# Layer 1's hidden-side products of chunks 0 to 2 as seven block products on quartered blocks

## The chip, the cores and the metric

The kernel runs on one core of a Trainium2 chip. The metric is the device time of one execution in microseconds (us), with all inputs in the chip's memory (HBM) at the start and the output there at the end. The kernel before has a median of 1414.64 us over 3 runs (1414.49 to 1414.83).

## The reference

Two layers are applied to x, 2048 rows by 512 columns. Each adds a Fourier mixing of the normalized rows, and then a small MLP with shifts along the sequence. Cut to what matters:

```python
def _A_ref(x, dft_seq_re, dft_seq_im, dft_hid_re, dft_hid_im):
    a = jnp.einsum("bsd,ed->bse", x, dft_hid_re)
    b = jnp.einsum("bsd,ed->bse", x, dft_hid_im)
    y = jnp.einsum("ts,bse->bte", dft_seq_re, a) - jnp.einsum("ts,bse->bte", dft_seq_im, b)
    return y

def _B_ref(x, w1, w2, w3, w4):
    h = _gelu(_layernorm(x, axis=-1) @ w1)
    hs = ...            # h with its four column groups shifted by +1, -1, +2, -2 rows, @ w2
    x1 = x + hs
    h2 = _gelu(_layernorm(x1, axis=-1) @ w3) @ w4
    return x1 + h2

x = A_x
for _ in range(2):
    x = x + _A_ref(_layernorm(x, axis=-1), ...)
    x = x + _B_ref(_layernorm(x, axis=-1), B_w1, B_w2, B_w3, B_w4)
```

The change concerns the product with the hidden-side matrices (`dft_hid_re`, `dft_hid_im`) in the second layer, which the kernel calls layer 1.

## The kernel before

**Numbers.** Every fp32 operand of a matmul is held as two numbers, a high part (a cast to fp32r by ScalarE, ACT) and a low part (the difference, by VectorE, DVE). A product is three matmuls on TensorE (PE), high by high, high by low and low by high; `mm3` issues them (lines 303 to 305). So each operand costs a cast on ACT and a subtraction on DVE ahead of its first use.

**Transform.** The rows are worked in four chunks c = 0 to 3 of 512. First come the products with the sequence-side matrices (`in_ws`), whose results are the real and imaginary blocks `re0, re1, im0, im1` in the tile `rr`, each 128 partitions by 2 by 512 columns, high and low part side by side. Then comes the product of these blocks with the hidden-side matrix `in_hs`. The sequence-side work of a chunk has two phases:

- The **x phase** (`x_phase`) has eight pairs k = 0 to 7, each with an even step 2k (12 matmuls of 512 columns, called the wide step in the prediction) and an odd step 2k + 1 (6 matmuls, the narrow step). Steps are numbered 0 to 15.
- The **y phase** (`y_phase`) has 16 steps of 12 matmuls.

The hidden-side products of chunk c - 1 stand in the x phase of chunk c, as eight pieces of 512 KB, in pairs given by the table `HAT`. `hid` does one piece: 2 x 2 products by `mm3`, 12 matmuls of 512 columns, into the banks `PD`. Four pieces make half of the chunk's rows, and `add_y` adds them to x and collects the row sums in the same DVE operation (line 607). Those of chunk 3 come after its y phase, by `hid` too.

**How operands come.** A list `items`, made before anything is issued, says in which order pieces of `in_ws` and `in_hs` are used. A piece is brought by a DMA that SyncE (SP) issues (line 223) into one of four raw buffers of 512 KB (two more, `wide`, toward the y phase). From there it goes to one of four ring slots of 1024 KB: `stage_one` casts the high part on ACT (line 247 for a whole piece, a "plain" item; for an odd step, a "one" item, a DVE difference comes first, line 249), and `stage_two` makes the low part on DVE (line 266). `stream` is called at each step and keeps the ring full, so DMAs, casts and low parts run up to four places ahead of PE. A raw buffer is free for the next DMA when its last reader is done, and a DMA that has to wait for that holds up all those behind it on SP.

**Other work in the x phase.** The table `late` maps a step number to pieces of work that `run_late` issues at that step: the sums and the high and low parts of the last chunk's `re` and `im` blocks, and the normalization sums of its rows. `hook(i)` loads x rows and stores results at fixed steps. Each engine works its own instructions in the order in which the program issues them.

**MLP.** `by_pairs` works two chunks at a time. `first_pair` does chunks 0 and 1. The second pair (chunks 2 and 3) in layer 0 is a loop over five rounds p, each with seven block products `prod` (banks b1, b6, b5, b2, b7, b4, b3 in turn out of four), whose sums `u, v, x, y` DVE adds. Between them `w4_part` does the product with w4, and the list `bg`, one entry at a time by `one()`, prepares the rows of layer 1. At a round's end `w3_load` brings the weight block (1792 KB) of the round after the next. In the next round, two sums read b4 and b3 of the round before it is over:

```python
            prod(b4, w, 6, "t4")
            add(v, b4, v, ALU.subtract)
            low2 = gelu_high(h4[2 * (p % 2) + 1], v)
            prod(b3, w, 2, "22")
            add(x, x, b3)
```

The banks are `bk[(2 + 7 * p + i) % 4]`, so b4 of a round is the bank that the third product of the next round writes.

## Time and profile before

| | before |
|---|---|
| median of 3 runs | 1414.64 us |
| the profiled execution | 1414.44 us |
| its span, first to last instruction | 1412.5 us |
| PE busy | 1407.2 us |
| DVE busy | 1190.1 us |
| ACT busy | 765.3 us |
| GpSimd (POOL) busy | 96.5 us |
| traffic with HBM | 260.70 MB read, 54.26 MB written, 223 GB/s |
| layer 1, x phase of chunk 1 | 792.77 to 847.17, 54.40 us |
| layer 1, y phase of chunk 1 | 847.17 to 890.70, 43.53 us |
| layer 0, MLP of chunks 2 and 3 (second pair) | 603.22 to 716.27, 113.05 us |

The profile is of one execution. A row of a group gives line, engine, operation, what is written and read, the shape, how many, the busy time and the mean ns of one, and the idle time ahead of them with what ended it. A row of a stretch of time gives the stretch, its length, and the busy time and number of instructions of PE, its weight loads (PEld), DVE, ACT and POOL, the clock that PE was granted (1.00 is full), the DMA share and GB/s. A row of the order of time gives the start, the duration and, in brackets, the idle time ahead with what ended it. Matmuls overlap: one shows 0.39 us at 512 columns, and the distance between starts is what it costs PE.

### The profile page before, as it was taken

What the parts mean: (1) busy time and instruction counts of PE and PEld (TensorE: products, weight loads), DVE (VectorE), ACT (ScalarE), POOL (GpSimd) and SP (SyncE); (2) the same over time, 40 slices, a digit from 0 to 9 for tenths busy, and PEclk for the clock granted to TensorE, in tenths of its full rate; (3) what the DMA queues carried; (4) which work ended last, traced back from release to release, by engine and by line L of the source; (5) the groups of instructions that cost most, each with busy time, mean ns of one, the idle gap of its engine ahead of it and who ended that gap; (6) DMA issues with size and microseconds to landing.
All of it is one profiled execution on the core that took longest, in us unless ns stands there. A gap on an engine that the chain in (4) does not pass through costs nothing.

```text
span 1412.5 us, 18484 instructions
## 1 busy us (share of the span) xinstructions
PE 1407.2 (100%) x6669; PEld 1181.7 (84%) x6669; DVE 1190.1 (84%) x1684; ACT 765.3 (54%) x1072; POOL 96.5 (7%) x105
## 2 busy tenths in 40 slices
PE   9999999999999999999999999999999999999998
PEld 8888888888888888988888888888888888899887
DVE  7988998999988789856789979879889788897776
ACT  6765565556566645434555544555555666454351
POOL 2100220400001100000000000000000020000000
PEclk9999999999999999999999999999999999999999
DMA  8878868778874848864656476565577457677864
GB/s 295 307 235 300 262 206 274 241 239 293 284 229 131 281 148 262 269 235 168 216 164 216 146 224 211 160 214 178 188 248 248 136 143 244 193 247 257 295 208 158
DMA packets 158907, 316.18 MB, mean 224 GB/s; under 512 B 10848, under 2 KB 78816, under 8 KB 156896
## 3 DMA queue, kind: packets, MB, share of 16 engines
q1 hardware_dynamic: 158816, 315.01, 67.8%
q8 instruction: 52, 0.85, 0.2%
q14 instruction: 39, 0.32, 0.1%
HBM read 260.70 MB, written 54.26 MB: 223 GB/s over the span
## 4 chain that ended last, share of the span: by engine, by line
PE 95%; DVE 3%; ACT 1%; issue 1%; DMA 0%; SPq 0%; POOL 0%; DVEq 0%; ACTq 0%; POOLq 0%
PE psd L303 10%; PE psd L304 10%; PE psd L305 10%; PE psa L303 8%; PE psa L305 8%; PE psa L304 8%; PE psb L303 7%; PE psb L304 7%; PE psb L305 7%; PE psc L304 7%; PE psc L303 7%; PE psc L305 7%; DVE rest L500 1%; DVE z3turned L643 1%; DVE uv L500 0%
## 5 line engine op out<-in xcount | busy, mean ns | idle before, releaser
L247 ACT CAST ring<-raw 128x1024 fp32r<-128x1024 f32 x127 | 132.6, 1051 | 70.4 <-PE psd L305 33.7
L266 DVE TENSOR_TENSOR ring<-raw,ring 128x1024 fp32r<-128x1024 f32 x126 | 153.3, 1219 | 14.3 <-ACT ring L247 14.3
L354 POOL TENSOR_TENSOR rows<-ve,mhalf 128x4 f32<-128x4 f32 x16 | 47.2, 2952 | 702.9 <-DVE ve L353 702.9
L303 PE MATMUL psd<-ring,rr 128*128 128x512 f32 x208 | 80.9, 389 | 0.0
L304 PE MATMUL psd<-ring,rr 128*128 128x512 f32 x208 | 80.9, 389 | 0.0
L305 PE MATMUL psd<-ring,rr 128*128 128x512 f32 x208 | 80.9, 389 | 0.0
L322 POOL TENSOR_TENSOR rs<-ve,mhalf 128x2 f32<-128x2 f32 (+2 forms) x33 | 28.4, 862 | 411.8 <-DVE nb L321 392.9
L266 DVE TENSOR_TENSOR ring<-ring1f,ring 128x512 fp32r<-128x512 f32 (+1 forms) x56 | 53.3, 952 | 2.2 <-ACT ring L254 1.4
L254 ACT CAST ring<-ring0f 128x1024 fp32r<-128x1024 f32 x28 | 29.5, 1054 | 43.9 <-DVE ring0f L253 43.7
L303 PE MATMUL psc<-ring,ay 128*128 128x512 f32 x128 | 49.8, 389 | 0.0
L304 PE MATMUL psc<-ring,ay 128*128 128x512 f32 x128 | 49.8, 389 | 0.0
L305 PE MATMUL psc<-ring,ay 128*128 128x512 f32 x128 | 49.8, 389 | 0.0
L303 PE MATMUL psb<-ring,ay 128*128 128x512 f32 x128 | 49.8, 389 | 0.0
L304 PE MATMUL psb<-ring,ay 128*128 128x512 f32 x128 | 49.8, 389 | 0.0
L305 PE MATMUL psb<-ring,ay 128*128 128x512 f32 x128 | 49.8, 389 | 0.0
L303 PE MATMUL psa<-ring,ay 128*128 128x512 f32 x126 | 49.0, 389 | 0.0
L304 PE MATMUL psa<-ring,ay 128*128 128x512 f32 x126 | 49.0, 389 | 0.0
L305 PE MATMUL psa<-ring,ay 128*128 128x512 f32 x126 | 49.0, 389 | 0.0
L303 PE MATMUL psd<-ring,ay 128*128 128x512 f32 x126 | 49.0, 389 | 0.0
L304 PE MATMUL psd<-ring,ay 128*128 128x512 f32 x126 | 49.0, 389 | 0.0
L305 PE MATMUL psd<-ring,ay 128*128 128x512 f32 x126 | 49.0, 389 | 0.0
L305 PEld LDWEIGHTS psd<-ring,rr 128*128 128x128 f32 x208 | 39.1, 188 | 8.1
(834 smaller groups left out, 4597.4 us busy)
## 6 DMA issues: line engine op xcount, KB each, us to landing
raw<-in_ws SPq DMA_DIRECT2D x183, 512.0 KB, 5.4
raw<-in_hs SPq DMA_DIRECT2D x56, 512.0 KB, 3.7
w3b<-w3d SPq DMA_DIRECT2D x11, 1792.0 KB, 8.3
w4r<-w4d SPq DMA_DIRECT2D x22, 512.0 KB, 3.4
un<-w4s SPq DMA_DIRECT2D x40, 256.0 KB, 4.1
un<-w4d SPq DMA_DIRECT2D x38, 256.0 KB, 4.2
x1d<-tmp SPq DMA_DIRECT2D x12, 512.0 KB, 6.9
xs<-x1d SPq DMA_DIRECT2D x12, 512.0 KB, 5.6
```

Of the source, the lines that this page charges most:

```text
L247: nc.scalar.copy(dest[:, a:b, 0], r[0][:, a:b])
L254: casts.append(lambda: nc.scalar.copy(dest[:, :, 0], lo))
L266: nc.vector.tensor_tensor(lo, src, hi.bitcast(F32), op=ALU.subtract)
L303: nc.tensor.matmul(o, lh, rh, start=first, stop=False, skip_group_check=more)
L304: nc.tensor.matmul(o, lh, rl, start=False, stop=False, skip_group_check=more)
L305: nc.tensor.matmul(o, ll, rh, start=False, stop=last, skip_group_check=more)
L322: nc.gpsimd.tensor_tensor(rs[:, :n], ve[:, :n], mhalf[:, 0, :n], op=ALU.pow)
L354: nc.gpsimd.tensor_tensor(rs, ve, mhalf[:, :, :2], op=ALU.pow)
L500: nc.vector.tensor_tensor(o, a, b, op=op)
L643: nc.vector.transpose(v, blocks_of(u))
```

## The change

In layer 1, the hidden-side products of chunks 0 to 2 are no longer eight `hid` pieces. The blocks `re0, re1, im0, im1` and the hidden-side matrix are each cut into a 2 x 2 of quarters, and the product of the 2 x 2 blocks is made by seven products in place of eight, after Strassen and Winograd. The operands are then not quarters alone but sums of them, which the code calls forms.

- **The products.** `form_product` does one: 4 x 2 calls of `mm3`, 24 matmuls of 256 columns (the two runs of 128 columns of a right form), into one of the two banks `PD`; the table `FORMS` gives the step ahead of which each stands, steps 5, 9, 10, 11, 12, 13 and 14 for products 2, 1, 5, 6, 3, 7 and 4. DVE adds each into x by `drain`, at once or at the step that `DRAINS` gives. The row sums that `add_y` took along are made by ACT (`row_sums`).
- **The left forms** (of `re` and `im`) are made by the `late` table of steps 1 to 12: ten sums (five before) and seven high and seven low parts (three of each before), each of 1024 columns.
- **The right forms** are the same for all chunks. They are made once, in layer 0's second MLP pair, from `in_hs`, in eight units: `right_load` (256 KB), `right_sums` (four DVE sums of 128 columns, and casts on ACT), `right_lows` (DVE) and `right_keep` (a store of 896 KB into the DRAM tile `hfd`). Units 2 and 3 stand in round 1, units 4 and 5 in round 2, unit 6 in round 3.
- **Bringing the right forms.** Forms 1, 5, 6 and 7 come as new "ready" items, by one DMA of 1024 KB from `hfd` straight into a ring slot, without cast or subtraction. Forms 2, 3 and 4 are brought by `bring_right` at steps 0, 9 and 11 into places of their own (form 2 in four DMAs of 256 KB, into the room of the two wide raw buffers, where left form 6 is made later).
- **Around it.** `wide` begins at step 13 instead of 11; from late in a y phase to step 14 the fourth raw buffer is kept out of use (`kept`); half of the x rows are loaded at step 3 instead of 4, and rows are stored at step 15 instead of 9; in chunk 3 the order in which rows are turned for the MLP is changed (`BACK`, `turn_one`); `high(im0)` and `low(im0)` leave the y phase of chunks 0 to 2.

The diff, cut to its core:

```diff
+FORMS = {5: 2, 9: 1, 10: 5, 11: 6, 12: 3, 13: 7, 14: 4}
+DRAINS = {2: 8, 1: 9, 5: 10, 6: 11, 3: 12}
+BY_HAND = {0: 2, 9: 3, 11: 4}
...
             for k in range(NP):
-                if c:
+                if c and not layer:
                     for h in range(NP):
                         if HAT[h] == k:
                             item("plain", piece(hs[HORDER[h % 4]]))
                 p = piece(ws[c, k][:, 2:4])
-                item("plain", p)
-                item("one", p, span=(0, 1))
+                for i, kind in enumerate(("plain", "one")):
+                    f = FORMS.get(2 * k + i) if c and layer else None
+                    if f and f not in BY_HAND.values():
+                        item("ready", f)
+                    item(kind, p, span=(0, 2 - i))
...
+        if kind == "ready":
+            to = in_forms(dest).rearrange("p u h w -> p (u h w)")
+            nc.sync.dma_start(to.bitcast(F32), hfd[RIGHT.index(ids[0])].rearrange("p u h w -> p (u h w)"))
+            state["one"] += 1
+            return
...
+    def form_product(c, n):
+        rh, rl = right_of(n)
+        hi, lo, _ = left_forms[n]
+        bank = PD[n in (2, 5, 3)]
+        new = n in (1, 2, 5)
+        for u in range(4):
+            for q in range(2):
+                v = slice(q * P, (q + 1) * P)
+                first = new and u == 0 and q == 0
+                o = bank[:, q * 2 * P : (q + 1) * 2 * P].rearrange("p (v w) -> p v w", v=2)
+                mm3(o, hi[:, u, v], lo[:, u, v], rh[:, u], rl[:, u], first, True, not first)
...
+        def drain():
+            add(x[:, :, cols], bank.rearrange("p (q w) -> p q w", q=2), x[:, :, cols])
...
+                    5: [left_sum(7)],
+                    6: [left_low(1), left_high(7)],
+                    7: [left_sum(5), left_sum(6), left_high(5), left_high(6)],
+                    8: [left_low(5)],
+                    9: [left_low(6), left_sum(3), left_high(3)],
+                    10: [left_low(3), left_high(4)],
...
+        def right_sums(u):
+            for o, a, b in ((4, 1, 0), (5, 3, 1), (1, 3, 4), (6, 2, 1)):
+                add(form_at(u, o), form_at(u, a), form_at(u, b), ALU.subtract)
+            for _, t in unit_room[u]:
+                nc.scalar.copy(t[:, :, 0].bitcast(F32R), t[:, :, 1])
+
+        def right_lows(u):
+            for _, t in unit_room[u]:
+                add(t[:, :, 1].bitcast(F32R), t[:, :, 1], t[:, :, 0], ALU.subtract)
...
+            if p in (1, 2):
+                right_sums(units[p][0])
             tiles = [(fs[0], h4[2])] if p == 0 else [(2 * p - 2 + i, h4[2 * ((p - 1) % 2) + i]) for i in range(2)]
-            for f, h in tiles:
+            for i, (f, h) in enumerate(tiles):
                 w4_part(acc1, f, h)
                 w4_load()
                 one()
+                if not i and p in (1, 2):
+                    right_lows(units[p][0])
+                if i == len(tiles) - 1 and units[p]:
+                    right_sums(units[p][-1])
...
             w3_load(NF // 2 + p + 2)
             one()
+            if units[p]:
+                right_lows(units[p][-1])
+            for n in units[p]:
+                right_keep(n)
+            for n in loads_at[p]:
+                right_load(n)
```

Where it moves instructions is seen at two places. The first is SP's queue of DMAs in the x phase of chunk 1, in layer 1. `raw` are the raw buffers, filled from the sequence-side (`in_ws`) or hidden-side (`in_hs`) matrix; `tmp<-x2d` are x rows. Before:

```order
367 L223 DMA raw_182<-in_hs 128x1024
368 L223 DMA raw_183<-in_ws 128x1024
369 L206 DMA tmp<-x2d 128x2x512
370 L223 DMA raw_180<-in_hs 128x1024
371 L206 DMA tmp<-x2d 128x2x512
372 L223 DMA raw_181<-in_hs 128x1024
373 L223 DMA raw_182<-in_ws 128x1024
374 L223 DMA raw_183<-in_hs 128x1024
375 L223 DMA raw_180<-in_hs 128x1024
376 L223 DMA raw_181<-in_ws 128x1024
```

After, from the same place on; `form60` and `form61` take form 2, the four transfers into `ring` are forms 1, 5, 6 and 7 in this order, and `all0` and `all1` take forms 3 and 4:

```order
389 L597 DMA form61_288<-hfd_103 128x4x128 x2
390 L232 DMA raw1_182<-in_ws 128x1024
391 L215 DMA tmp_104<-x2d_74 128x2x512
392 L232 DMA raw2_183<-in_ws 128x1024
393 L215 DMA tmp_104<-x2d_74 128x2x512
394 L258 DMA ring1_175<-hfd_103 128x2048
395 L232 DMA raw0_181<-in_ws 128x1024
396 L258 DMA ring3_179<-hfd_103 128x2048
397 L258 DMA ring1_175<-hfd_103 128x2048
398 L593 DMA all0_278<-hfd_103 128x8x256
399 L232 DMA raw1_182<-in_ws 128x1024
400 L258 DMA ring0_173<-hfd_103 128x2048
```

The eight `in_hs` pieces are gone. Row 395 is the `in_ws` piece of the x phase's last pair, k = 7, which waits for a raw buffer; the transfers of forms 5 (row 396), 6 and 3 stand behind it.

The second place is DVE's queue in round 2 of layer 0's second MLP pair, from the sum `add(y, v, b5)` to `add(x, x, b3)`. `rest` are the tiles u, v, x and y, `ps...` the banks, `h` a split gelu output, and `ax2f` rows of layer 1. Before:

```order
752 L500 TENSOR_TENSOR rest_244<-rest_242,psa_245 128x512
753 L671 TENSOR_TENSOR h_206<-tmp,h_206 128x512
754 L393 TENSOR_TENSOR ax2f<-xs_147 128x2x256
755 L394 TENSOR_TENSOR ax2f<-xs_147 128x256
756 L500 TENSOR_TENSOR rest_242<-psd_252,rest_242 128x512
757 L500 TENSOR_TENSOR rest_243<-rest_243,psa_245 128x512
```

After; `righthx` and `hc67` hold unit 4 of the right forms, `cell` and `junk` unit 5:

```order
770 L529 TENSOR_TENSOR rest7_252<-rest5_250,psa0_253 128x512
771 L814 TENSOR_TENSOR h40_207<-tmp_104,h40_207 128x512
772 L529 TENSOR_TENSOR hc67_3896<-righthx_3898 128x128 x2
773 L529 TENSOR_TENSOR righthx_3898<-righthx_3898,hc67_3896 128x128
774 L529 TENSOR_TENSOR hc67_3896<-righthx_3898 128x128
775 L413 TENSOR_TENSOR ax2f_126<-xs2_148 128x2x256
776 L414 TENSOR_TENSOR ax2f_126<-xs2_148 128x256
777 L529 TENSOR_TENSOR righthx_3898<-righthx_3898 128x4x128
778 L529 TENSOR_TENSOR hc67_3896<-hc67_3896 128x3x128
779 L529 TENSOR_TENSOR cell_3895<-cell_3895 128x128 x3
780 L529 TENSOR_TENSOR junk_69<-cell_3895 128x128
781 L529 TENSOR_TENSOR rest5_250<-psd1_260,rest5_250 128x512
```

The sums of units 4 and 5 and the low parts of unit 4 now stand on DVE between the sum `add(y, v, b5)` (752, now 770) and the sum `add(v, b4, v)` (756, now 781), which frees bank b4.

More of the change, by code (lines that the diff above doesn't have):

```diff
@@ L195, in spectral_mlp_kernel @@
     held = {i: None for i in range(len(raw_at))}
-    state = {"wide": False, "hold": False, "dma": 0, "one": 0, "two": 0, "use": 0, "made": 0, "done": 0, "limit": 0, "load": w_pieces[0]}
+    state = {"wide": False, "kept": 0, "hold": False, "dma": 0, "one": 0, "two": 0, "use": 0, "made": 0, "done": 0, "limit": 0, "load": w_pieces[0]}
     x_left = [(0, 1), (1, 1)] + [(j, 2) for j in range(2, NT, 2)]
@@ L453, in spectral_mlp_kernel, with name_blocks @@
     re0s, re1s, im0s, im1s = (f[:, :, 1] for _, f in (re0, re1, im0, im1))
+    re_im = [both(f"all{i}", RR + i * 8 * CH, KD, 2, CH) for i in range(2)]
+    apart = re0, re1, im0, im1
+    together = [[t[:, 2 * h : 2 * h + 2] for t in pair] for pair in re_im for h in range(2)]
+    def name_blocks(blocks):
+        nonlocal re0, re1, im0, im1, re0s, re1s, im0s, im1s
+        re0, re1, im0, im1 = blocks
+        re0s, re1s, im0s, im1s = (f[:, :, 1] for _, f in blocks)
     mid = [rr[i // 2][i % 2].rearrange("p t r (h d) -> p (t r h) d", h=2) for i in range(4)]
@@ L510, in x_phase @@
             first, last = k == 0, k == NP - 1
-            while c and h < NP and HAT[h] == k:
+            if seven and 2 * k in FORMS:
+                form_product(c - 1, FORMS[2 * k])
+            while c and not seven and h < NP and HAT[h] == k:
                 s = stream()
@@ L531, in x_phase @@
                 cast_held()
+            if seven and 2 * k + 1 in FORMS:
+                form_product(c - 1, FORMS[2 * k + 1])
             s = stream()
@@ L560, in y_phase @@
                         nc.scalar.copy(X1[:, i], PD[i])
-                    high(im0)
+                    if not seven:
+                        high(im0)
             else:
-                if k == NP - 2:
+                if k == NP - 2 and not seven:
                     low(im0)
@@ L1698, in spectral_mlp_kernel @@
         state["limit"] = w_items[layer]
+        if layer:
+            name_blocks(together)
         zs = {}
@@ L1855, in hook @@
                     turn_in(ztf[0])
-            y_phase(c, hook)
+            y_phase(c, hook, layer and c < NC - 1)
             state["wide"] = False
```

171 lines of the change are left out of this document (149 added, 22 removed).

## The prediction

> **What bounds the kernel now.** I read the page first, then the busy times by stage, then TensorE's instructions in order of time around the products that are replaced. In the page I took the busy times of the engines and the head of the chain that ended last:
>
> ```profile
> PE 1407.2 (100%) x6669; PEld 1181.7 (84%) x6669; DVE 1190.1 (84%) x1684; ACT 765.3 (54%) x1072; POOL 96.5 (7%) x105
> ...
> PE 95%; DVE 3%; ACT 1%; issue 1%; DMA 0%; SPq 0%; POOL 0%; DVEq 0%; ACTq 0%; POOLq 0%
> ```
>
> TensorE (PE) is busy in all of the span, and 95% of the chain is its own work. So a matmul less is time less, as long as nothing new makes PE wait. What could make it wait is seen by stage. The next rows are layer 1's transform of chunk 1 (x phase, then y phase) and the x phase of chunk 3; the columns are stage, length, then busy time and instructions of PE, weight loads, VectorE (DVE), ScalarE (ACT) and GpSimd, the granted clock, the DMA share and GB/s:
>
> ```profile
> 792.77:847.17 54.40, 54.40 (x241) 45.05 (x240) 43.13 (x52) 27.75 (x36) 1.20 (x2) 1.00 0.63 200
> 847.17:890.70 43.53, 43.53 (x194) 36.04 (x193) 39.92 (x40) 23.81 (x30) 1.34 (x2) 1.00 0.57 185
> ...
> 988.62:1043.02 54.40, 54.40 (x242) 45.05 (x241) 43.13 (x52) 29.18 (x38) 1.21 (x2) 1.00 0.66 220
> ```
>
> PE never pauses here and its clock is whole. DVE has 11 us free of 54 in an x phase, and under 4 of 43 in a y phase. The hidden-side products that the change replaces stand in the x phases of chunks 1 to 3 (each does those of the chunk before), where DVE has room.
>
> **The matmuls.** Per chunk, `hid` issued 8 pieces x 2 x 2 x 3 = 96 matmuls of 512 columns; seven products of 4 x 2 x 3 matmuls are 168 of 256 columns. The price of the first is the distance from the start of a run of 24 of them to what follows; that of the second comes from the one stage that has such matmuls, layer 0's first MLP pair. Start, busy time, engine, line, shape:
>
> ```profile
> 807.74 0.39 PE L303 MATMUL psd<-ring,rr 128*128 128x512 f32 x1
> ...
> 813.17 0.39 PE L303 MATMUL psc<-ring,ax 128*128 128x512 f32 x1
> ```
>
> ```profile
> 550.13 0.28 PE L303 MATMUL psb<-un,hr 128*128 128x256 f32 x1
> ...
> 551.20 0.28 PE L303 MATMUL psd<-un,hr 128*128 128x256 f32 x1
> ```
>
> ```profile
> 553.00:600.00 47.00, 47.00 (x417) 47.00 (x416) 43.31 (x62) 24.55 (x38) 0.00 (x0) 1.00 0.82 267
> ```
>
> 24 of 512 columns take 5.43 us, 0.2265 each. In the steady stretch 416 of 256 columns take 47.0 us, 0.113 each: half. So a chunk's products fall from 96 x 0.2265 = 21.7 us to 168 x 0.113 = 19.0, that is 2.7 us, and 8.2 us for three chunks. The weight load before each matmul (0.19 us long in the trace) still overlaps, since the spacing is 0.113.
>
> The Trainium skill, "TensorE: Matmul & The Clock Gate", section "Back-to-back issue gap", speaks against many small matmuls: a matmul has a fixed part of about 2.5 ns beside its N/2.4 ns. By its formula (an estimate) the chunk falls from 20.7 to 18.3 us, three chunks gain 7.1 us and not 8.2, and the sum below would be 1411.1; the measured spacings, 0.2265 and half of it, show no such fixed part, so it gets no chance of its own.
>
> What the small ones do cost is the change of shape. From 550.13 to 551.20 nine matmuls took 1.07 us, 0.119 each, 0.05 us more than at the steady rate, and the way back is seen here:
>
> ```profile
> 603.22 0.39 PE L303 MATMUL psd<-b,w4r 128*128 128x512 f32 x1
> ...
> 605.97 0.39 PE L303 MATMUL psd<-b,w4r 128*128 128x512 f32 x1
> ```
>
> Twelve of 512 columns took 2.75 us, 0.03 over 12 x 0.2265. Every form product stands alone between wide matmuls, so there are 21 ways in and 21 back: 21 x 0.08 = 1.7 us given back. The forms are streamed as two runs of 128 columns, which no row shows; I put it at nothing. Bounds for both: 0, and 3.1 if all 24 matmuls of a product ran at 0.119.
>
> **DVE and ACT in the x phase.** The durations are those of chunk 1's x phase, by shape:
>
> ```profile
> L266 DVE TENSOR_TENSOR ring<-raw,ring 128x1024 fp32r<-128x1024 f32 x15 | 18.2, 1221 | 3.5 <-ACT ring L247 3.5
> L607 DVE SCALAR_TENSOR_TENSOR tmp<-psd,tmp 128x512 f32<-128x512 f32 x4 | 2.7, 692 | 3.3 <-PE psd L305 3.3
> ...
> L247 ACT CAST ring<-raw 128x1024 fp32r<-128x1024 f32 x14 | 14.6, 1052 | 11.8 <-PE psd L305 5.6 <-PE psb L305 4.6 <-ACT ring L247 1.2
> L345 ACT ACTIVATE junk<-tmp,rows 128x512 bf16<-128x512 f32 x2 | 1.4, 721 | 0.0
> ```
>
> and DVE's order of time at two places of it:
>
> ```profile
> 788.10 0.68 DVE L249 TENSOR_TENSOR ring1f<-raw 128x512 f32<-128x512 f32 x1
> 788.70 1.22 DVE L266 TENSOR_TENSOR ring<-raw,ring 128x1024 fp32r<-128x1024 f32 x1
> ...
> 820.79 2.36 DVE L266 TENSOR_TENSOR ring<-raw,ring 128x1024 fp32r<-128x1024 f32 x2
> ```
>
> A 1024-wide DVE operation is 1.22 us, one every 1.14 back to back (two in 2.36); a 512-wide one holds the queue 0.6. Gone are 8 low parts of `in_hs` pieces; added are 4 low parts (7 for 3) and 5 sums (10 for 5): one more, 1.1 us. Seven drains of 512 replace 4 `add_y`: about 1.5 us more (7 x 0.61 against 4 x 0.69). DVE goes from 43.1 of 54.4 us to some 45.8 of 51.7. ACT loses 8 casts, gains 4 and 4 row sums: about level. The cover is DVE's idle time; without it these 2.6 us a chunk would be PE's.
>
> Where order matters, I followed each left form from the `late` table to its product, taking PE's x phase as wide step 2.72 us, narrow step 1.36, product 2.72. The tightest is product 5's low part (slot 8, product at 25.84 us of the phase): DVE's queue, reckoned through by these durations, ends it at about 24.7. The drain of product 7 has the narrow step 13 (1.36 us) before product 4 writes the same bank, and takes 0.7. Both hold, by about a microsecond and by half of one.
>
> **The right forms' transfers.** A form is 1024 KB, read into a ring slot as soon as the step four places before it has been multiplied. Products 1, 5 and 6 have three steps, 6.8 us, from the slot's release to their use; product 7 has 9.5. Rows of the transfers, KB and median us from issue to landing, the last one for a single transfer at 636.08 us with nothing else in flight:
>
> ```profile
> w3b<-w3d SPq DMA_DIRECT2D x11, 1792.0 KB, 8.3
> w3b<-w3d SPq DMA_DIRECT2D x6, 1024.0 KB, 5.6
> zt0f<-zd SPq DMA_DIRECT2D x4, 1024.0 KB, 6.4
> un<-w4s SPq DMA_DIRECT2D x40, 256.0 KB, 4.1
> rt<-xtd SPq DMA_DIRECT2D x2, 1024.0 KB, 10.1
> ```
>
> ```profile
> w3b<-w3d SPq DMA_DIRECT2D x1, 1792.0 KB, 7.0
> ```
>
> At 5.6 us products 1 and 6 are in time. Product 5 is not quite: on SP its transfer stands behind the `in_ws` piece of the last pair, which waits until DVE has formed the difference of step 9 from that buffer. From step 1's start at 2.72 up to that difference DVE has twelve 1024-wide operations and six 512-wide ones in its queue (the `late` table and the ring), 12 x 1.14 + 6 x 0.6 = 17.3 us, so SP is free at about 20.0, though the slot is at 19.04. Then 512 + 1024 KB land together: between 5.6 us (1024) and 7.0 (1792), 6.5 by length, at 26.5, and PE wants them at 25.84. The queue's gaps and starts may move this by half a microsecond; I take 0.5 us a chunk, 1.5 in all; bounds 0, and 1.6 a chunk at the 8.3 us of the crowded row.
>
> DMA traffic rises by 7 x 1024 - 8 x 512 = 3072 KB a chunk, from 200 GB/s x 54.4 us = 10.9 MB to about 14 MB in 51.7 us, 270 GB/s; the trace shows 332 GB/s over 13 us elsewhere:
>
> ```profile
> 1364.00:1377.00 13.00, 13.00 (x59) 10.78 (x58) 8.82 (x15) 7.85 (x14) 0.00 (x0) 1.00 0.97 332
> ```
>
> **Making the right forms.** Eight units stand in layer 0's second MLP pair; each adds 4 DVE sums of 128 columns, the low parts of 7 x 128 and as wide a cast on ACT. DVE's rows of that stage for 256 and 768 columns:
>
> ```profile
> 618.40 0.42 DVE L394 TENSOR_TENSOR ax0f<-tmp 128x256 f32<-128x256 f32 x1
> ...
> 622.52 0.96 DVE L419 TENSOR_TENSOR ax<-ax0f,ax 128x768 fp32r<-128x768 f32 x1
> ```
>
> A unit is 4 sums of under 0.42 each (I take 0.2) and 896 columns in one or two low parts (1.1), 1.9 us, 15 for all eight. The stage, in slices of 10 us, has that room on DVE:
>
> ```profile
> 640.00:650.00 10.00, 10.00 (x46) 8.29 (x45) 5.71 (x14) 4.14 (x6) 0.89 (x2) 1.00 0.45 164
> 650.00:660.00 10.00, 10.00 (x46) 8.28 (x45) 8.12 (x16) 4.44 (x8) 0.89 (x2) 1.00 0.59 213
> ```
>
> The danger is not that work but the wait for its input. Units 4 and 5 are loaded at the end of round 1 (636.1 us) behind a 1792 KB weight block (7.0 us) and two stores of 896 KB. Before, the block ran at this rate while it was in flight:
>
> ```profile
> 640.00:641.00 1.00, 1.00 (x6) 0.84 (x5) 0.97 (x4) 0.00 (x0) 0.00 (x0) 1.00 1.00 430
> ```
>
> The stores and unit 4 are 2 x 896 + 256 KB, 2.1 MB, 4.9 us at 430 GB/s: unit 4 is there at 636.1 + 7.0 + 4.9 = 648.0, and DVE, which reaches its sums at about 645, stands. Unit 5's load waits until the stores have landed (0.6 us sooner, 647.4) and takes 4.1 us: 651.5. Behind both on DVE is the sum `add(v, b4, v)`, which reads the bank that the third product of the next round writes:
>
> ```profile
> 649.69 0.69 DVE L500 TENSOR_TENSOR rest<-psd,rest 128x512 f32<-128x512 f32 x1 [2.25 <-PE psd L305]
> ...
> 653.57 0.39 PE L303 MATMUL psd<-bt,w3b 128*128 128x512 f32 x1
> ```
>
> It starts at 649.69 now; behind unit 5's four sums of 0.2 it would end at 651.5 + 0.8 + 0.7 = 653.0, with PE due at 653.57. I take 0.6 us for it (bounds 0, and 5 if the block and the stores go at the 8.3 us of the crowded row and round 4 inherits the delay).
>
> **Sum.** -8.2 + 1.7 + 1.5 + 0.6 = -4.4 us against the profiled execution, 1414.44 us (span 1412.5 and 1.9 around it): 1410.0. The median of the runs shown is 0.2 above that execution, 1414.64; I leave that out.
>
> **Rivals.** (a) All hidden: PE waits nowhere and only the change of shape costs: -8.2 + 1.7, 1407.9; with that free too, 1406.3. For it: the deadlines miss by under a microsecond. Chance 0.2. (b) The MLP wait takes most of the gain: 3 there and 0.8 a chunk at product 5 leave -8.2 + 1.7 + 3 + 2.4 = -1.1, 1413.3 (1412 to 1415). For it: DVE is in order and stands before a bank that PE needs. Against: half a microsecond of slack by the lone block's 7.0 us. Chance 0.18. (c) Slower: the forms come late every time. If a 1024 KB form takes 9 us, between the rows of 6.4 and 10.1, products 1, 5 and 6 wait 2.2 us each, 6.6 a chunk, 20 in all: -8.2 + 1.7 + 20 = +13, 1428. It decides from 7.5 us a form on (0.7 x 9 = 6.5). For it: 270 GB/s on average with rows of 10.1. Against: forms are contiguous by partition like the block that went at 7.0 for 1792 KB. Chance 0.06. (d) That the matmuls aren't replaced is excluded by the instruction order: PE has 216 more, 3 x 72.
>
> **Numbers.** My forecast has 0.56, (a) 0.2, (b) 0.18, (c) 0.06. The range from 1406.3 to 1413.6 takes in (a), the forecast and the better part of (b). 0.2% is 2.8 us, about what a measurement of this kernel can tell from no change: below 1411.8 lie the forecast (nearly all) and (a), 0.74; (b) and the rest of the forecast are the same, 0.2; (c) 0.06.
>
> **What would show it.** Right: x phases of chunks 1 to 3 some 2 us shorter each, products of 24 at 2.72 to 2.8 us, and a wait of PE at product 5 alone, with a transfer as the one that came last. A wait at the third product of rounds 2 to 4 of the MLP pair (released by DVE) shows (b). Waits at products 1 and 6 for transfers show (c). Wrong would be a spacing over 0.12 us in the products, or waits in the y phases, where DVE has least room.

## The result, and the profile after

The changed kernel takes 1428.37 us (median of 4 runs, 1426.65 to 1428.52), the one before 1414.57: a ratio of 1.0094, 95% interval 1.0077 to 1.0112; by the medians it is 13.8 us slower. The profiled execution took 1428.52 us (span 1426.6). The forecast was 1410.0 with a range of 1406.3 to 1413.6, so it missed in sign as well as in size. Rival (c) had 1428 for its time, but that number is a coincidence, as the waits below show.

The page first, busy times, the head of the chain, and the transfers of right forms into ring slots (KB, median us to landing):

```profile
PE 1406.5 (99%) x6885; PEld 1187.2 (83%) x6885; DVE 1209.7 (85%) x1728; ACT 763.9 (54%) x1096; POOL 104.5 (7%) x105
...
PE 84%; DVE 7%; DMA 5%; issue 2%; ACT 1%; SPq 0%; POOL 0%; DVEq 0%; POOLq 0%; ACTq 0%
...
ring<-hfd SPq DMA_DIRECT2D x12, 1024.0 KB, 6.7
```

PE's share of the chain fell from 95% to 84%, and DVE and DMAs now hold 12%. Its busy time is only 0.7 us less, though 288 matmuls of 512 columns gave way to 504 of 256. PE's waits, grouped by what released them (total, times, longest); before, the view held the one row of `ident` alone:

```profile
PE psd L323 <- DVE tmp L529: 5.3, 3, 2.2
PE psd L323 <- DMA ring<-hfd: 5.1, 4, 1.8
PE psd L323 <- DVE rest L529: 1.9, 2, 1.2
PE psd L146 <- POOL ident masks.py:199: 1.4, 1, 1.4
PE psd L325 <- DVE h L814: 1.2, 1, 1.2
PE psc L324 <- DVE ring L286: 1.0, 1, 1.0
```

Three kinds of new waits: `tmp L529` is a drain (x phases), `ring<-hfd` a right form's transfer (x phases), and the other three stand in the MLP pair and at the start of layer 1. The stages after, in the columns of the first rows of the prediction (second MLP pair; x phase of chunk 0; x and y phase of chunk 1; x phases of chunks 2 and 3):

```profile
603.68:720.68 117.00, 113.90 (x501) 93.20 (x499) 91.25 (x184) 58.47 (x95) 6.97 (x12) 1.00 0.81 280
720.68:755.02 34.34, 33.32 (x145) 26.74 (x144) 33.07 (x53) 20.32 (x29) 3.21 (x4) 1.00 0.55 178
798.54:855.33 56.79, 53.60 (x314) 46.82 (x313) 45.22 (x49) 22.10 (x28) 0.00 (x0) 1.00 0.74 244
855.33:898.85 43.52, 43.52 (x194) 36.05 (x193) 39.11 (x42) 26.95 (x41) 3.98 (x4) 1.00 0.57 190
898.85:955.52 56.67, 53.60 (x314) 46.84 (x312) 45.21 (x49) 22.09 (x28) 0.00 (x0) 1.00 0.74 244
999.04:1056.96 57.92, 53.59 (x314) 46.83 (x312) 45.21 (x49) 23.49 (x30) 0.00 (x0) 1.00 0.76 257
```

and of before for the first two of these:

```profile
603.22:716.27 113.05, 113.05 (x501) 93.40 (x499) 77.67 (x139) 52.01 (x80) 6.59 (x12) 1.00 0.60 210
716.27:749.25 32.98, 32.94 (x145) 26.95 (x144) 31.61 (x51) 20.44 (x29) 3.21 (x4) 1.00 0.55 181
```

The x phases of chunks 1 to 3 are longer by 2.4, 2.3 and 3.5 us, the MLP pair by 3.95, chunk 0's x phase by 1.4; the y phases are as before. That is 13.5 of the 14.1 us by which the span grew; most of the rest lies ahead of these stages. PE's busy time in an x phase (53.60 of 56.79) is only 0.8 us under the 54.40 of before.

**The products.** One product, from its first matmul to what follows it:

```profile
832.63 0.28 PE L323 MATMUL psd<-ring,form 128*128 128x256 f32 x1
...
835.50 0.39 PE L323 MATMUL psa<-ring,ax 128*128 128x512 f32 x1
```

24 matmuls took 2.87 us, 0.12 each, not 0.113. A product that PE had to wait for takes 2.94 to 2.98.

**Product 5** waits for its right form. SP's queue around it (start, time, line, transfer), and the product:

```profile
819.35 0.33 SPq L232 DMA_DIRECT2D raw<-in_ws  x1
820.07 4.03 SPq L258 DMA_DIRECT2D ring<-hfd  x2
```

```profile
824.75 0.39 PE L325 MATMUL psa<-ring,ax 128*128 128x512 f32 x1
826.94 0.36 PE L323 MATMUL psd<-ring,all 128*128 128x256 f32 x1 [1.80 <-DMA ring<-hfd]
```

The form's transfer goes out at 820.07, right behind the pair's piece, and the product begins 6.9 us later, 2 us after the step before it was through (824.75 and the 0.23 of one wide matmul).

**Product 4** waits for product 7's drain. DVE's queue ahead of it, and PE:

```profile
838.04 0.68 DVE L286 TENSOR_TENSOR ring<-ring1f,ring 128x512 fp32r<-128x512 f32 x1
844.04 1.23 DVE L611 TENSOR_TENSOR all<-all1f,all 128x1024 fp32r<-128x1024 f32 x1 [5.32 <-DMA all<-hfd]
...
847.52 0.68 DVE L529 TENSOR_TENSOR tmp<-psd,tmp 128x512 f32<-128x512 f32 x1
```

```profile
848.25 0.39 PE L323 MATMUL psd<-all 128*128 128x256 f32 x1 [1.34 <-DVE tmp L529]
```

DVE stands 5.3 us before the low part of left form 4 (`all<-all1f,all`), released by the transfer of right form 4 (`all<-hfd`). The two lie in the same tile, `all1`, in different columns. Behind that low part come an older drain, the work for the next step, and at 847.52 product 7's drain, whose bank product 4 writes.

**The MLP pair.** SP, DVE and PE in round 2:

```profile
643.40 2.21 SPq L1211 DMA_DIRECT2D righthx<-in_hs  x2
651.63 0.42 SPq L999 DMA_DIRECT2D w3b<-w3d  x1
```

```profile
650.39 0.65 DVE L529 TENSOR_TENSOR hc<-righthx 128x128 f32<-128x128 f32 x2 [2.51 <-DMA righthx<-in_hs]
...
654.68 0.68 DVE L529 TENSOR_TENSOR rest<-psd,rest 128x512 f32<-128x512 f32 x1
```

```profile
655.42 0.50 PE L323 MATMUL psd<-bt,w3b 128*128 128x512 f32 x1 [1.23 <-DVE rest L529]
```

Unit 4's load goes out at 643.40 and its sums start at 650.39. The sum that frees bank b4 starts at 654.68, where it started at 649.69 before, and the third product of the next round waits 1.23 us for it.

### The profile page after: what moved, and what is told of

It is laid out like the page before. It is cut to its first block, busy times and chain, and to the rows that moved or that the text cites. A ratio compares the mean times of both kernels' runs of the same rounds, so it can differ in the third digit from the quotient of the medians.

```text
span 1426.6 us, 19044 instructions
## 1 busy us (share of the span) xinstructions
PE 1406.5 (99%) x6885; PEld 1187.2 (83%) x6885; DVE 1209.7 (85%) x1728; ACT 763.9 (54%) x1096; POOL 104.5 (7%) x105
## 4 chain that ended last, share of the span: by engine, by line
PE 84%; DVE 7%; DMA 5%; issue 2%; ACT 1%; SPq 0%; POOL 0%; DVEq 0%; POOLq 0%; ACTq 0%
PE psd L323 9%; PE psd L325 9%; PE psd L324 9%; PE psa L323 7%; PE psa L325 7%; PE psa L324 7%; PE psb L324 6%; PE psb L323 6%; PE psb L325 6%; PE psc L324 6%; PE psc L325 6%; PE psc L323 6%; DVE ring L286 2%; DMA ring<-hfd 1%; DMA all<-hfd 1%
## 5 line engine op out<-in xcount | busy, mean ns | idle before, releaser
L264 ACT CAST ring<-raw 128x1024 fp32r<-128x1024 f32 x103 | 107.6, 1050 | 40.1 <-PE psd L325 15.4
L286 DVE TENSOR_TENSOR ring<-raw,ring 128x1024 fp32r<-128x1024 f32 x102 | 124.3, 1220 | 3.9 <-ACT ring L264 3.7
L374 POOL TENSOR_TENSOR rows<-ve,mhalf 128x4 f32<-128x4 f32 x16 | 53.5, 3344 | 704.2 <-DVE ve L373 704.2
L286 DVE TENSOR_TENSOR ring<-ring1f,ring 128x1024 fp32r<-128x1024 f32 (+1 forms) x53 | 51.3, 968 | 2.2 <-ACT ring L271 1.4
L323 PE MATMUL psb<-ring,ay 128*128 128x512 f32 x128 | 49.8, 389 | 0.0
L323 PE MATMUL psc<-ring,ay 128*128 128x512 f32 x128 | 49.8, 389 | 0.0
L323 PE MATMUL psd<-ring,ay 128*128 128x512 f32 x126 | 49.0, 389 | 0.0
L323 PE MATMUL psa<-ring,ay 128*128 128x512 f32 x126 | 49.0, 389 | 0.0
L286 DVE TENSOR_TENSOR ring<-ring3f,ring 128x1024 fp32r<-128x1024 f32 (+1 forms) x47 | 47.2, 1004 | 0.4
L286 DVE TENSOR_TENSOR ring<-ring2f,ring 128x1024 fp32r<-128x1024 f32 (+1 forms) x40 | 42.4, 1060 | 4.0 <-ACT ring L267 2.2
L851 DVE TENSOR_TENSOR rg<-gt,rg 128x512 fp32r<-128x512 f32 x32 | 22.0, 689 | 28.0 <-ACT rg L850 28.0
L324 PE MATMUL psc<-ring,ax 128*128 128x512 f32 x112 | 43.9, 392 | 1.0 <-DVE ring L286 1.0
```

What stands on the lines that cost most here:

```text
L264: nc.scalar.copy(dest[:, a:b, 0], r[0][:, a:b])
L286: nc.vector.tensor_tensor(lo, src, hi.bitcast(F32), op=ALU.subtract)
L323: nc.tensor.matmul(o, lh, rh, start=first, stop=False, skip_group_check=more)
L324: nc.tensor.matmul(o, lh, rl, start=False, stop=False, skip_group_check=more)
L374: nc.gpsimd.tensor_tensor(rs, ve, mhalf[:, :, :2], op=ALU.pow)
L851: nc.vector.tensor_tensor(lo, src, hi.bitcast(F32), op=ALU.subtract)
```

## The experiments

Ratios are to the kernel before, measured on the same chip. An expectation was written before its run. Each run keeps the profile of one execution, and stages differ between executions: in the profiles of experiments 1, 2, 7, 8, 9 and 13, which leave the making of the right forms as it is, the MLP pair is 3.0 to 4.4 us longer than before, against 3.95 in the changed kernel.

**1. The low part of left form 4 ahead of form 4's transfer.**

```diff
-                    11: [left_low(7)],
-                    12: [left_low(4)],
+                    11: [left_low(7), left_low(4)],
```

> The low part of left form 4 is issued on DVE at step 11, ahead of form 4's transfer, instead of at step 12 behind it. Theory (DVE stands before that low part until the transfer has landed, 5.3 us in chunk 1, and product 7's drain behind it is late, so PE waits at product 4): DVE's idle time there goes, PE's waits at product 4 (1.3, 1.7 and 2.2 us) go, time 1428.4 - 5.3 = 1423.1 us. Rival (the transfer itself is too late, or DVE's queue is full anyway): product 4 then waits for the transfer of form 4 or still for the drain, and at most 1.5 us come back, 1427 or more.

Measured: 1423.29 us, ratio 1.0067 (1.005 to 1.0084). DVE and PE at the same place, chunk 1:

```profile
835.32 1.22 DVE L611 TENSOR_TENSOR form<-form7f,form 128x1024 fp32r<-128x1024 f32 x1
836.46 1.22 DVE L611 TENSOR_TENSOR all<-all1f,all 128x1024 fp32r<-128x1024 f32 x1
```

```profile
845.54 0.39 PE L325 MATMUL psa<-ring,ax 128*128 128x512 f32 x1
845.77 0.28 PE L323 MATMUL psd<-all 128*128 128x256 f32 x1
```

The low part runs without a wait, product 4 starts 0.23 us behind the start of the last wide matmul, which is its normal distance, and no wait for a drain is left in PE's waits. By the medians 5.1 us came back against 5.3 expected; in the profiled executions the three x phases are 6.3 us shorter than the changed kernel's. Form 4's own transfer is not late: the rival falls.

**2. Form 5's transfer ahead of the last pair's piece.** The piece waits until the form is issued.

```diff
+        if items[min(state["one"], len(items) - 1)][:2] == ("ready", (5,)):
+            return
         while state["dma"] < (state["load"] if upto is None else upto):
...
             state["one"] += 1
+            issue_dma()
             return
```

> Form 5's transfer is issued on SP ahead of the last pair's in_ws piece instead of behind it; nothing else moves. Theory (the transfer is late because SP stands before the piece until DVE has made the difference of step 9): it is issued about 1.5 us sooner, PE's waits at product 5 (1.8, 1.2 and 1.6 us, and the step before, 4.7 in all) fall to 0.5 or less each, time about 1424.5. Rival (the transfer takes as long as the waits want because the DMA engines are full): it lands no sooner than before, or the piece of the last pair is late in its place and steps 14 and 15 wait, 1427.5 to 1429.

Measured: 1427.17 us, ratio 1.0089 (1.0074 to 1.0104), which can't be told from the changed kernel's 1.0094. The profiled execution took 1425.50, 3.0 under the changed kernel's, and PE's waits in it were:

```profile
PE psd L326 <- DVE tmp L532: 6.0, 3, 2.3
...
PE psd L326 <- DMA ring<-hfd: 1.3, 3, 0.5
```

The waits for right forms fell from 5.1 to 1.3 us, as the theory has it: those at product 5 are gone, the 1.3 stand at product 1. Those for product 7's drain rose from 5.3 to 6.0, since in chunk 1 PE lost at product 4 some 0.9 us of what it gained at product 5. Another loss is not a wait at all. Behind the wait at product 4 of chunk 1 (2.28 us, over at 846.78) stand these two stretches; the clock is the third number from the end:

```profile
846.78:848.30 1.52, 1.52 (x12) 1.52 (x13) 1.52 (x2) 0.36 (x1) 0.00 (x0) 1.00 0.60 189
848.30:851.70 3.40, 3.40 (x16) 3.21 (x15) 0.77 (x3) 0.69 (x1) 0.00 (x0) 0.51 0.97 336
```

For 3.4 us PE was granted half its clock, and the matmuls there took about 1.5 us longer than at their usual spacing. Without that stretch this execution would have been at about 1424.0, near the 1424.5 expected; the changed kernel's profile has none. So the edit does what the theory says. Why the median shows only 1.2 us of it stays open, since the other executions have no profile. The runs below with both edits took 1419.48 (experiment 7), 1418.46 (experiment 8) and 1419.08 us (experiment 12), 9 to 10 us under the changed kernel.

**3. In the MLP pair, the sums of a round's last unit behind the sum that frees b4; unit 4 loaded a round sooner.**

```diff
-        loads_at = ((2, 3), (4, 5), (6,), (), ())
+        loads_at = ((2, 3, 4), (5,), (6,), (), ())
...
-                if i == len(tiles) - 1 and units[p]:
-                    right_sums(units[p][-1])
...
             add(v, b4, v, ALU.subtract)
+            if units[p]:
+                right_sums(units[p][-1])
             low2 = gelu_high(h4[2 * (p % 2) + 1], v)
```

> In the MLP pair unit 4 is loaded a round sooner, and the sums of units 1, 3, 5 and 6 stand behind the sum that frees bank b4 instead of ahead of it. Theory (DVE stands before a unit's input with the sum for the bank behind it): PE's waits of 1.2 and 0.6 us in rounds 3 and 4 go; the wait of 1.2 at the end, from a full queue of DVE, stays or halves; 1428.4 - 1.9 = 1426.5, down to 1425.3. Rival (the 15 us of added DVE work are too many for the stage wherever they stand): the waits move to other places and the time stays within 0.7 us of 1428.4.

Measured: 1426.25 us, ratio 1.0086 (1.0071 to 1.0101); by the interval again not told from the changed kernel. In the profile PE's wait for `rest` on DVE fell from 1.9 to 0.2 us, and a new one of 0.7 us, `PE psa L323 <- ACT rest L1267`, took its place: ACT now stood longer for a unit's sums, which its casts need, with the round's first bank behind them. The pair was 3.25 us longer than before, which lies within the 3.0 to 4.4 of the profiles that leave this stage as it is. So the wait on DVE nearly went and a smaller one took its place; that the stage became shorter is not shown.

**4. The DVE work of making the right forms left out.** The sums give way to three copies on ACT, the low parts to nothing, so the products multiply other numbers.

> The DVE work that makes the right forms is left out: no sums and no low parts (three copies on ACT stand for the sums, so that what is stored has been written); loads and stores stay. It prices that DVE work. Theory: the MLP pair falls by 4.0 us to its length of before, 113.05, and the x phase of layer 1's chunk 0, 1.4 us longer now because of the last unit on DVE, to 32.98: 1428.4 - 5.4 = 1423.0. Rival (the loads and stores, not DVE, cost the time): the pair stays over 116 us and the time over 1427.

Measured: 1429.44 us, ratio 1.0105 (1.0089 to 1.012). The stretch of the MLP pair, and PE's wait in it:

```profile
603.40:720.30 116.90, 113.88 (x501) 93.27 (x500) 74.98 (x137) 63.03 (x119) 6.59 (x12) 1.00 0.81 279
```

```profile
PE psa L323 <- ACT rest L1266: 2.4, 2, 1.4
```

DVE's busy time there fell from 91.25 to 74.98 us, and the pair stayed 3.85 us over before. That goes against the theory as I had put it: 16 us less work on DVE did not shorten the stage. But the copies put ACT where DVE had stood, before the units' loads, and PE waited for ACT instead. Since the edit moved the wait as well as removing work, it doesn't price the making; experiment 6 does.

**5. The two edits of the x phase and a spread-out making together.**

```diff
-        loads_at = ((2, 3), (4, 5), (6,), (), ())
+        loads_at = ((2, 3, 4), (5,), (6,), (), ())
...
                     right_lows(units[p][0])
-                if i == len(tiles) - 1 and units[p]:
-                    right_sums(units[p][-1])
+                    right_keep(units[p][0])
...
             gelu(hcs[2 * p], x)
+            if units[p]:
+                right_sums(units[p][-1])
             w3_load(NF // 2 + p + 2)
...
-        for n, f in ((0, right_load), (5, right_sums), (6, right_lows), (8, right_keep)):
+        for n, f in ((0, right_load), (6, right_sums), (8, right_lows), (9, right_keep)):
```

> The two edits of the first two experiments together (low part of left form 4 ahead of its transfer; form 5's transfer ahead of the last pair's piece), and the making of the right forms spread out: unit 4 loaded a round sooner, units 2 and 4 stored as soon as they are made, the sums of units 1, 3, 5 and 6 behind both sums that free PE's banks and behind the round's gelus, unit 7's sums one step and its low parts two steps later. Theory (each of the waits is a queue standing before a transfer, and they add): x phases 1.0 to 1.3 us shorter than before each, MLP pair and chunk 0's x phase 1 to 2 us longer than before instead of 5.4: 1414.4 - 3.5 + 1.5 = 1412.4, between 1411.5 and 1414. Rival (the work and traffic added are too many, and waits only move): 1416 to 1420.

Measured: 1417.19 us (11 runs), ratio 1.0019 (1.0009 to 1.003): 11 us better than the changed kernel and still slower than before. In the profile the pair is 1.2 us over before and the x phases of chunks 1 to 3 differ by +0.4, -1.2 and 0.0, but chunk 0's x phase is 2.9 us over, twice as much as without the shift of unit 7:

```profile
PE psd L326 <- DMA ring<-hfd: 2.3, 4, 0.9
PE psc L327 <- DVE ring L289: 1.9, 2, 1.0
```

Unit 7's low parts, put later, came to stand on DVE among the last operations ahead of the first pieces of layer 1 (713.11, the first piece's low part at 714.71).

**6. The right forms not made at all.** The two edits of the x phase; seven copies of 1024 KB from `in_ws` fill `hfd`, so other numbers are multiplied.

> The same two edits in the x phase, and the right forms are not made at all: seven copies of 1024 KB from the sequence-side matrix fill their place, so the products multiply other numbers; loads, sums, casts, low parts and stores of the eight units are gone. It prices the making as a whole. Theory: MLP pair and chunk 0's x phase as before, x phases as in the repaired kernel: 1414.4 - 3.5 = 1410.9. Rival (the making is not what lengthens these two stages): 5 us more, 1416.

Measured: 1413.40 us, ratio 0.9991 (0.9982 to 1.0). Chunk 0's x phase and the MLP pair are as before to 0.01 us; the work ahead of the pair is 0.6 longer. So the making is what lengthens these stages. But the gain left is 1.0 us, where I expected 3.5: the products cost more than I thought, and waits of 1.1 us for right forms stay.

**7. The two halves of the bank in turn outside.** Experiments 7 to 9, 12 and 13 all have the two edits of the x phase, and the making as in the changed kernel.

```diff
-        for u in range(4):
-            for q in range(2):
+        for q in range(2):
+            for u in range(4):
```

> The two edits in the x phase, the making as in the changed kernel, and the loop over the two halves of the bank is put outside the loop over the operand's four rows, so that 12 matmuls in a row write the same half instead of 3. Theory (the products take 0.119 to 0.124 us a matmul because of their shape or their operands, not because of the bank's half): products still 2.8 to 2.95 us, time as low part and form 5 together make it, 1417. Rival (changing the half costs): products fall to 2.72 us, 3 us in all, 1414.

Measured: 1419.48 us, ratio 1.0032 (1.002 to 1.0044). The products take 2.82 to 2.98 us as before. The half of the bank is free.

**8. One run of 256 moving columns instead of two of 128.** High and low parts are mixed.

```diff
-            return of_two
+            return [pair[0] for pair in form6]
...
-        return s[:, :, :, :P], s[:, :, :, P:]
+        return s[:, :, 0], s[:, :, 1]
...
-                o = bank[:, q * 2 * P : (q + 1) * 2 * P].rearrange("p (v w) -> p v w", v=2)
+                o = bank[:, q * 2 * P : (q + 1) * 2 * P]
```

> The two edits in the x phase, the making as in the changed kernel, and the moving operand of each product is read as one run of 256 columns instead of two of 128 (other numbers are multiplied: high and low parts are mixed). Theory (the two runs cost the 0.006 us a matmul over 0.113): products fall from 2.87 to 2.75 us or less, 2.5 to 3 us in all, 1414.5. Rival (runs are free): products stay at 2.85 or more, 1417.

Measured: 1418.46 us, ratio 1.0024 (1.0014 to 1.0034). The products stay at 2.85 to 2.98 us (product 2 at 2.82). The theory falls, the rival holds: the two runs cost nothing that shows.

**9. Product 2 three times over**, its result counted three times.

```diff
-        for u in range(4):
+        for u in [0, 1, 2, 3] * (3 if n == 2 else 1):
```

> The two edits in the x phase, the making as in the changed kernel, and the loop of product 2 runs three times over the same operands, 72 matmuls of 256 columns in a row instead of 24 (the extra ones count its result three times). Theory (the matmuls behind a change of shape are slow, however the operand lies): from some place in the run on, they follow each other at 0.113 us as in the MLP, and the run takes about 2.82 + 48 x 0.113 = 8.2 us. Rival (something in these products' operands or places makes each 0.118 to 0.12): 72 x 0.1175 = 8.5 us.

Measured: 1433.01 us, ratio 1.0132 (1.0114 to 1.0151). The run of 72 in chunk 1:

```profile
808.61 0.28 PE L326 MATMUL psd<-form,all 128*128 128x256 f32 x1
...
817.09 0.39 PE L326 MATMUL psa<-ring,ax 128*128 128x512 f32 x1
```

8.48 us for 72, 0.118 each. The matmuls don't speed up behind the first ones: the theory falls, and the spacing isn't a matter of standing right behind the change of shape.

**10. The low parts of the units on GpSimd**, with experiment 5's edits but unit 7's old steps.

```diff
-                add(t[:, :, 1].bitcast(F32R), t[:, :, 1], t[:, :, 0], ALU.subtract)
+                nc.gpsimd.tensor_tensor(t[:, :, 1].bitcast(F32R), t[:, :, 1], t[:, :, 0], op=ALU.subtract)
```

> The repaired kernel with unit 7's steps back where the change has them, and the low parts of the right forms' units made by GpSimd instead of DVE. Theory (DVE's queue is what the making lengthens; a unit's 1.2 us of low parts there is over half of it): chunk 0's x phase about 0.7 us over before instead of 2.9, MLP pair 0.6 to 1.2 over, 1414.5 to 1415. Rival (the sums and the casts on ACT are what is late, or GpSimd is so slow that the normalization sums on it come late): 1416.5 or more.

Measured: 1415.95 us, ratio 1.0015 (1.0006 to 1.0024), between what the two expect; in the profiled execution (1417.82) the pair was 2.1 us over before and chunk 0's x phase 1.8.

**11. The sums and casts on GpSimd too.**

```diff
-                add(form_at(u, o), form_at(u, a), form_at(u, b), ALU.subtract)
+                nc.gpsimd.tensor_tensor(form_at(u, o), form_at(u, a), form_at(u, b), op=ALU.subtract)
...
-                nc.scalar.copy(t[:, :, 0].bitcast(F32R), t[:, :, 1])
+                nc.gpsimd.tensor_copy(t[:, :, 0].bitcast(F32R), t[:, :, 1])
```

> As the run before, and the sums and the casts of the units on GpSimd too, so that the making touches neither DVE nor ACT. Theory: both stages come to within 0.6 us of before, as in the run without making, 1413.5. Rival (GpSimd is in order too: the normalization sums behind the units on it are late, ACT and then DVE wait for them): the MLP pair is 2 us or more over before and the time 1416 or more.

Measured: 1416.12 us, ratio 1.0017 (1.0008 to 1.0026). The pair is 0.7 us over before, but chunk 0's x phase still 1.6, though neither DVE nor ACT does any of unit 7. The normalization sums, which the rival names, explain little of it: ACT stood 3.6 us for them around there, against 3.2 in experiment 6. GpSimd's and DVE's work at the place of unit 7, ahead of chunk 0's x phase:

```profile
702.18 0.93 POOL L1219 CAST cells<-cells 128x896 fp32r<-128x896 f32 x1
703.20 2.13 POOL L1223 TENSOR_TENSOR cells<-cells 128x896 fp32r<-128x896 f32 x1
```

```profile
699.38 0.95 DVE L416 TENSOR_TENSOR ax4f<-tmp 128x512 f32<-128x512 f32 x1
...
703.72 2.16 DVE L816 TENSOR_TENSOR h<-hc,h 128x512 fp32r<-128x512 f32 x1 [1.92 <-POOL cells L1219]
...
706.67 0.68 DVE L816 TENSOR_TENSOR h<-hc,h 128x512 fp32r<-128x512 f32 x1
```

The same DVE operation takes 2.16 us while GpSimd's low part runs and 0.68 after it. (The cast of `h` that it waited for was ACT's, over at 703.63.) With three shorter ones, each 0.27 longer beside GpSimd's sums, that is about 2.3 us, and DVE reaches layer 1's first difference 2.4 us later, counted from the pair's start, than in experiment 6. That chunk 0's x phase gets its 1.6 us from this is argued from the order of the queue, not shown by a run.

**12. One operand of the products changed at a time** (each with other numbers), to find what makes 0.118.

```diff
...
+                b = PD[q] if n == 2 else bank
+                o = b[:, q * 2 * P : (q + 1) * 2 * P].rearrange("p (v w) -> p v w", v=2)
+                lh, ll, a, b = hi[:, u, v], lo[:, u, v], rh[:, u], rl[:, u]
+                if n == 1:
+                    a = b = rh[:, 0]
+                if n == 5:
+                    ll = lh
+                if n == 6:
+                    lh = ll = hi[:, 0, :P]
+                if n == 4:
+                    for l, r in ((lh, a), (lh, b), (ll, a)):
+                        nc.tensor.matmul(o, l, r, start=True, stop=True, skip_group_check=True)
+                    continue
...
```

> A look at the spacing of the products, base as in the run by output halves but in the changed loop order. Each product changes one thing, and its numbers with it: product 2 writes its two halves to two banks in turn; product 1 reads the same 256 moving columns throughout; product 5 loads its high weights in place of its low ones; product 6 loads the same weights every time; product 4 doesn't accumulate; products 3 and 7 stay. Theory (the 0.118 belongs to 256 columns in this place and no operand of it): all stay at 2.82 to 2.98 us. Rival (one operand's place costs it): that product falls to 2.72 to 2.75, and names the cause.

Measured: 1419.08 us, one execution; all products between 2.82 and 2.98 us. None of these changes lowers the price.

**13. The narrow steps as 12 matmuls of 256 columns.**

```diff
-            mm_half(PA, ax[k][:, 0], s[:, 0], first, last)
+            for i in range(2):
+                for hh in (slice(0, 2 * P), slice(2 * P, 4 * P)):
...
+                    mm3(PA[i][:, hh], a[:, 0, w], a[:, 1, w], r[:, 0, hh], r[:, 1, hh], first and not hh.start, True, not (first and not hh.start))
```

> The narrow steps of all x phases, 6 matmuls of 512 columns, are issued as 12 of 256 on the same operands; the products stay. Theory (any short run of 256 columns among wide ones pays 0.118 a matmul): a narrow step takes 12 x 0.118 + 0.03 = 1.45 us, 0.09 more, 5 us in all over 56 of them. Rival (only the products' operands pay): 12 x 0.113 = 1.36, the time stays.

Measured: 1423.19 us, one execution. One narrow step in chunk 1 of layer 1, first step behind the last wide matmul and what follows it:

```profile
804.45 0.39 PE L328 MATMUL psb<-ring,ax 128*128 128x512 f32 x1
...
806.11 0.40 PE L326 MATMUL psc<-ring,ax 128*128 128x512 f32 x1
```

From 804.68 (804.45 and the 0.2265 of one wide matmul) to 806.11 are 1.43 us for 12, 0.119 each, and each undisturbed x phase of layer 0 became 0.78 us longer. On other operands, in another place, 256 columns cost the same 0.119. The theory holds: it isn't a matter of the products' operands.

## Why the prediction was wrong

Forecast and measurement by terms, against the profiled executions (us). The waits are read from PE's order of time, from the end of the step before to the product's start, together with what the product then takes over the 2.87 us of one that did not wait; the matmuls' term is what is left.

| term | forecast | measured |
|---|---|---|
| matmuls with the change of shape, three x phases | -6.5 | -4.7 |
| waits at product 1 | 0 | +1.4 |
| waits at product 5 | +1.5 | +5.4 |
| waits at product 4 | 0 | +6.1 |
| MLP pair | +0.6 | +4.0 |
| chunk 0's x phase | 0 | +1.4 |
| elsewhere, most of it ahead of the pair | 0 | +0.5 |
| sum | -4.4 | +14.1 |

**The matmuls: the size was off.** The step that failed is "416 of 256 columns take 47.0 us, 0.113 each: half", with the change of shape as 0.08 us for each product. The nine matmuls at 0.119 that I quoted were read as the cost of a change, over after 0.05 us; they were the price of the shape here, and 24 of them are 2.86, which I had only as the bound 3.1 (21 x 0.15). That bound left out the way back of 0.03, so the 3.5 us lost against the 8.2 lie even beyond it. The runs of 72 (0.118) and of 12 (0.119), on the operands of a product and on those of a narrow step, gave that price too. What lets layer 0's first MLP pair reach 0.113 behind its first matmuls stays open; the moving runs, the bank's halves, two banks in turn, accumulation and the choice of operands, each changed in one experiment or one product, left the price as it was.

The Trainium skill, "TensorE: Matmul & The Clock Gate", section "LDWEIGHTS (loading the stationary operand)", puts the load of 128 columns at P/1.2 ns, about 107 ns by an estimate from it, about as long as the 0.113 us of a matmul of 256 columns. The trace doesn't show that figure: it lists each load with 0.19 us, one starting every 0.12. That load and matmul are both near the bound, and neither hides the other's slips, would fit 0.119; no run here separates the two.

**Product 4: the step that failed is "Both hold, by about a microsecond and by half of one".** I reckoned DVE's queue by durations alone. The low part of left form 4, which the `late` table puts at step 12, waits for form 4's transfer, issued at step 11 into the same tile, and the drain stands behind it. The code has both in quarters of one tile; I asked of each transfer whether its product would get it in time, and not who else writes that tile. So the drain ended 1.5 to 2.4 us after PE wanted the bank, not half a microsecond before. Experiment 1 shows the cause: one line moved, and 5.1 us came back.

**Product 5: mechanism right, size off.** As forecast, the form's transfer stood behind the last pair's piece. I had SP free 20.0 us into the phase and the form landed at 26.5. SP issued the piece at 20.8 (819.35 - 798.54) and the form 0.7 behind it, since DVE had stood twice for half a microsecond before a cast of ACT and SP's row of the issue has 0.33 us; the transfer took 6.9 instead of 6.5, and 1.4 to 2.0 us were missing instead of 0.5. Experiment 2 removed the waits at product 5 by the order of two transfers. Product 1's small waits (0.2 to 0.6) are of the same kind.

**The MLP pair: mechanism right, size off by its first step.** I let the loads of units 4 and 5 be issued at 636.1, "at the end of round 1". Unit 4's went out at 643.40: on SP it stands behind the store of unit 3, which waits for unit 3's low parts on DVE. With the sums at 650.39 instead of 648.0, the sum for b4 ended 1.3 us after PE wanted the bank. Smaller waits follow, 0.7 us for a bank and 1.2 at the pair's end; that they stem from this one is not shown. I didn't cost unit 7 at all beyond its DVE time. Its sums and low parts stand on DVE at 704 to 710 us, ahead of chunk 0's x phase, in which DVE was busy for 31.61 of 32.98 us before and can make up little. So unit 7 is the likely cause of the 1.4 us there, but no run takes it away alone. Experiment 6 shows that both stages owe their length to the making as a whole. Experiment 5, with the same work on DVE at other places, brought the pair from 3.95 to 1.2 us over before, outside the 3.0 to 4.4 of the unchanged order: there the order decides more than the amount. Experiments 3, 4, 10 and 11 show such waits moving to ACT and to GpSimd.

**Rivals.** (b) had the right place in the MLP, but too little. (c) is refuted in spite of its 1428: a form took 6.7 us in the median of all, not 9, products 6 and 7 never waited for theirs, and the largest single cost was a wait for a drain that no rival had.

**The whole.** With the two edits of the x phase the change comes to 1418.5 to 1419.5, with the making spread out as well to 1416 to 1417, and even with right forms for nothing to 1413.4, ratio 0.9991 (0.9982 to 1.0). No version here beats the kernel before by a measurable amount. The gain of seven products for eight was 1.6 us a chunk at 0.119 a matmul, the way back included, where the forecast had 2.2; what is left of it goes into the remaining waits and the making.

## What to carry to other kernels

Follow a queue by what each instruction waits for, not by durations alone: in this kernel a transfer into a tile held up a writer of other columns of that tile that was issued behind it, and with it all that stood behind that writer. When a change halves the width of matmuls, price the narrow ones by a row from among wide ones, take the higher spacing seen as the price and not as a transient, and see what is left of the gain. Before an edit is judged by the time of a few executions, look in its profile for stretches at a lower granted clock and at how much unchanged stages vary: here one such stretch cost 1.5 us, half as much as the edit around it brought.

## What the runs showed of the hardware

- Matmuls of 256 columns cost 0.118 to 0.119 us in the x phases against 0.113 in the long stretch of the first MLP pair, at a granted clock of 1.00 in both.
- Behind some waits of PE the granted clock fell to about half for 3 to 4 us, at a cost of about 1.5 us: once in the profile of experiment 2, twice each in those of experiments 3 and 4, once in that of experiment 12, starting 0 to 2 us behind a wait of 1.8 to 2.5 us. Other waits as long had no such stretch behind them (2.24 us in chunk 3 of the changed kernel); no profile whose longest wait is 1.5 us or less has one. What decides is not shown.
- A DVE operation with two inputs in SBUF was held up by GpSimd: 2.16 us instead of 0.68 for 128x512 beside a GpSimd subtraction of 2.13 us. The Trainium skill, "SBUF — State Buffer", section "Who interferes with whom", says that such an instruction contends with a GpSimd one that reads SBUF; the trace of experiment 11 agrees.
- Moving side work from DVE to an idle GpSimd brought no gain that can be told: 1416.12 us, ratio 1.0017 (1.0008 to 1.0026), can't be told from the 1417.19 us, 1.0019 (1.0009 to 1.003), with that work on DVE and ACT.
